# Query features scaled by the ratio of their two sums, in a two-layer linear-attention and gated-MLP kernel

## The chip, the core and the metric

The kernel runs on one core of a Trainium2 chip, as one launch. The metric is the device time of that launch in microseconds. Five engines work side by side, each through its own queue in order: TensorE (PE, matmuls; its weight loads are shown as PEld), VectorE (DVE), ScalarE (ACT), GpSimd (POOL), and SyncE (SP), which here issues transfers. An engine that waits for a semaphore holds up everything behind it in its queue.

## The reference

Two rounds of attention block and MLP block on x of 2048 tokens x 512, all in bf16. Cut to what matters:

```python
def _A_ref(x, wqkv, w_phi, wo):                      # H = 32 heads of Dh = 16
    q, k, v = split(x @ wqkv)
    pq = jnp.einsum("bhsd,hdf->bhsf", q, w_phi)
    pk = jnp.einsum("bhsd,hdf->bhsf", k, w_phi)
    phi_q = jnp.concatenate([_softmax(pq, axis=-1), _softmax(-pq, axis=-1)], axis=-1)
    phi_k = jnp.concatenate([_softmax(pk, axis=-1), _softmax(-pk, axis=-1)], axis=-1)
    kv = jnp.einsum("bhsf,bhsd->bhfd", phi_k, v)
    z  = jnp.einsum("bhsf->bhf", phi_k)
    num = jnp.einsum("bhqf,bhfd->bhqd", phi_q, kv)
    den = jnp.einsum("bhqf,bhf->bhq", phi_q, z)[..., None] + 1e-6
    return (num / den) reshaped to (B, S, D) @ wo
def _B_ref(x, W_gate, W_up, W_down):                 # F = 1376
    gate = relu(x @ W_gate); return (gate * (x @ W_up)) @ W_down
x = x + _A_ref(_layernorm(x), ...); x = x + _B_ref(_layernorm(x), ...)   # twice
```

Each row of a softmax has 16 entries. The output of a query is a quotient in which phi_q stands above and below.

## The kernel before

The 2048 tokens are 16 tiles of 128 rows. x stays in SBUF (`X`) from the first load to the last store, and so do all the weights. At the start `w_phi` is made block diagonal (`Wblk`, line 409, DVE) and folded into the key and query parts of `wqkv` (`fold`, lines 430 to 453): weights are turned (`turn`, line 440), copied (`wT`), multiplied by `Wblk` (line 448) and copied into `Wk2` and `Wq2` (`W2`). One matmul group then gives p itself.

For each of the two layers:

- `norm_A` (480): row statistics on DVE, their Ln and Exp on ACT, scaled rows `xn`, turned by a transposing transfer (`turn`, 461) or by PE (466).
- Keys, per tile (`Keys.begin` and `finish`, 531 to 578): `K` on PE (535); exp(p) and exp(-p) on ACT into the two halves of `ek` (538); 64 row sums of 16 entries on DVE (`sk`, 546); 1/sum as Exp(-Ln) on ACT (555, 558); the scaling of `ek`, two instructions of 512 columns on POOL or DVE (`halves`, 505 to 519, recorded under line 509); `V` on PE (541) with a copy `vext` by ACT or DVE (425, 426); `kvz` on PE (570), which adds the tile to the sums over all tokens in the one PSUM tile `q`.
- `build` (580): DVE masks these sums into `R`, which every query needs.
- Queries, per tile (`query`, 594 to 613): `Q` on PE (597), exp(p) and exp(-p) on ACT (600), 64 sums on DVE (`sq`, 603), Ln and Exp of all 64 on ACT (606, 608), the scaling of both halves (`phq`, two instructions of 512 columns, line 509 again), and a transposing transfer on SP (`fq`, 611) that waits for both.
- `attend` (616): `erq` on PE (622), the reciprocal of the denominator (`rden`), the product `o` on DVE (636), its transposition `oT`, `proj` on PE (645), and x plus it on DVE with row sums (`resS`, 649).
- `mlp` (655), in blocks of 1, 2 or 4 tiles: centred rows `xc` on DVE (665), turned into `xnTB`; `G` and `Up` on PE (722), relu on ACT (`rg`, 726), the product `hT` on DVE straight from PSUM (739) or after an ACT copy (741, 730), `down` on PE (762), x plus it on DVE (769), and the store in layer 1 (833).

What runs when is not found by a scheduler on the chip. Every step is an `Op` in a list; `ORDER` (181) is a written-out permutation of the list, and each engine's queue is that order cut down to its own steps. `PLACE` (152) says, bit by bit, which of a step's two engines is taken where it has an `alt`; `SLOTS` (158) names the buffer that each step takes. `IDLE` (169) says how many matmuls on zeros (line 419) PE does ahead of its first steps, on top of the eight of `warm`. Pools that matter here: six PSUM tiles `b` for all projections, 21 tiles `ek`, 5 `vext`, 4 `sk`, 4 `sq`, 7 `fq`.

Work of layer 1's keys stands among the MLP of layer 0, and PE does in all 8 + 6 matmuls on zeros, 512 for the four attention projections, 1,691 for the MLP, and the rest for sums, queries and turns.

Of the kernel before, what the change touches and what calls it, by code (L numbers as in the profile page):

```python
# [8 lines left out]
P = 128  # L9
# [133 lines left out]
class K:  # L143
# [9 lines left out]
    "0101110100000000001100000100110001000011010001111000000011001101010101001001001000101001111111011010"  # L153
    "1011110000000100000001001101000000000111011001011111010111000101001100000101111101001100001101010100"
    "1111111110101010010001000011000100000000101100101010100001001100011100010000110011001101000110111001"
    "010110010110111001110100110100000"
)
SLOTS = (
    "0001425210034050000151131234202310332121143404550125d3104c02302b3020a12113g533004002394131703202e141"
    "5i022124504f013k03583226105214413624335a011h100b033c05053623122j214910170400020501131002000245011020"  # L160
    "2500001142021002010100203200101143020002012105002004314023104g13300215112012320410311e34110200400450"
    "10205113120513d5100i42221240121321402422031200151030231042100142131004133610104f33242541002510104203"
    "51101520500512052130201550414201515300804024k2232c4020121152143124212004023502a533344112050010024104"
    "02024213011055002220j4203h05133317362b222f1506242i013a114023391638231c343e352k221d014g10011500020514"
    "0010124302000012011021450000121302100024010021050012201000011011521101530431102000005112025421011101"
    "0213125200125020013101050032154203115143114220221100253415210511200211401013403005210402213013222420"
    "500210300512431510432512113015114024105320310110512400202"
)
IDLE = (
    0, 0, 0, 0, 0, 0, 0, 0, 0, 0, 2, 0, 4, 0, 0, 0, 0, 0, 0, 0, 0,  # L170
# [108 lines left out]
def kernel(  # L279
# [11 lines left out]
    def new(name, shape, dt=BF16):  # L291
        return sb.tile([P] + shape, dt, name=name)
# [47 lines left out]
    def op(eng, cost, due, emit, deps=(), takes=(), uses=(), name="", **kw):  # L340
        o = Op(eng, cost, due, emit, deps, takes, uses, name, **kw)
        ops.append(o)
        return o
# [535 lines left out]
```

## Time and profile before

| what | value |
|---|---|
| three runs | 377.31 us median (377.04 to 377.71) |
| span of the profiled execution, first to last instruction | 375.3 us |
| DVE, ACT and POOL busy, 10 to 60 us | 49.8, 48.2 and 36.2 of 50 us |
| DVE, ACT and POOL busy, 66 to 200 us | 103.7, 65.5 and 15.5 of 134 us |
| DVE, ACT and POOL busy, 200 to 260 us | 55.9, 45.0 and 36.9 of 60 us |
| DVE, ACT and POOL busy, 260 to 372 us | 62.8, 39.0 and 2.2 of 112 us |

The page gives the profiled execution its span alone; the runs' times are 1.7 to 2.4 us longer, 2.0 us at the median, which is what lies around the span. PE's busy share is near 100% in nearly every stretch, and since its matmuls overlap (a 512-column matmul is shown with 379 ns, but the next one starts 216 ns later) busy time alone doesn't tell lost time; counts of matmuls times the distance of their starts do. The same holds in small for DVE and ACT, whose instructions overlap by about a tenth of a microsecond.

### The profile page before, as it was taken

What the parts mean: (1) busy time and instruction counts of PE and PEld (TensorE: products, weight loads), DVE (VectorE), ACT (ScalarE), POOL (GpSimd) and SP (SyncE); (2) the same over time, 40 slices, a digit from 0 to 9 for tenths busy, and PEclk for the clock granted to TensorE, in tenths of its full rate; (3) what the DMA queues carried; (4) which work ended last, traced back from release to release, by engine and by line L of the source; (5) the groups of instructions that cost most, each with busy time, mean ns of one, the idle gap of its engine ahead of it and who ended that gap; (6) DMA issues with size and microseconds to landing.
All of it is one profiled execution on the core that took longest, in us unless ns stands there. A gap on an engine that the chain in (4) does not pass through costs nothing.

```text
span 375.3 us, 7459 instructions
## 1 busy us (share of the span) xinstructions
PE 364.6 (97%) x2793; PEld 216.6 (58%) x2833; DVE 285.1 (76%) x596; ACT 209.7 (56%) x553; POOL 93.5 (25%) x91
## 2 busy tenths in 40 slices
PE   8989997999999999999999999999999999999996
PEld 4534454868554554466476555587745444558585
DVE  6999999999998673685767999999994755543322
ACT  6989999746464532265155499973425323414031
POOL 0377984341010102001004269774000000000000
PEclk9999999999999999999999999999999999999999
DMA  8858844769814221012020102968664120211110
GB/s 256 191 139 175 312 58 85 123 113 132 164 36 84 47 53 31 11 25 56 9 56 2 29 2 57 141 93 142 143 132 85 31 56 2 56 29 51 42 51 30
DMA packets 93444, 31.21 MB, mean 83 GB/s; under 512 B 85248, under 2 KB 92384, under 8 KB 93408
## 3 DMA queue, kind: packets, MB, share of 16 engines
q1 hardware_dynamic: 92992, 30.34, 39.5%
q8 instruction: 22, 0.36, 0.4%
q10 hardware_dynamic: 416, 0.39, 0.3%
q14 instruction: 14, 0.11, 0.1%
HBM read 7.91 MB, written 2.10 MB: 27 GB/s over the span
## 4 chain that ended last, share of the span: by engine, by line
PE 90%; ACT 6%; DVE 1%; POOL 1%; issue 1%; DVEq 0%; another core or an unknown queue 0%
PE b L722 37%; PE b L762 20%; PE b L645 7%; PE b L541 6%; PE b L535 6%; PE b L597 6%; PE b L698 3%; PE q L622 2%; PE q L570 2%; ACT ek L600 1%; POOL ek L509 1%; ACT ek L538 1%; PE q L419 1%; DVE sq L603 1%; ACT hT L425 1%
## 5 line engine op out<-in xcount | busy, mean ns | idle before, releaser
L722 PE MATMUL b<-xnTB,wgu 128*128 128x128 bf16 (+2 forms) x1200 | 149.6, 279 | 0.0
L722 PEld LDWEIGHTS <-wgu 128*128 128x128 bf16 x1200 | 97.1, 98 | 43.6
L509 POOL TENSOR_TENSOR ek<-ek,sk 128x512 bf16<-128x512 bf16 x47 | 51.0, 1109 | 135.5 <-ACT sk L558 108.2
L726 ACT ACTIVATE gu<-b 128x512 bf16<-128x512 f32 (+1 forms) x83 | 47.8, 580 | 64.9 <-PE b L722 64.6
L762 PE MATMUL b<-wd,hT 128*128 128x512 bf16 (+2 forms) x350 | 81.3, 372 | 0.7
L762 PEld LDWEIGHTS <-hT 128*128 128x128 bf16 (+1 forms) x363 | 34.6, 98 | 35.9 <-DVE hT L739 0.2
L509 POOL TENSOR_TENSOR ek<-ek,sq 128x512 bf16<-128x512 bf16 x38 | 42.0, 1127 | 32.6 <-ACT sq L608 18.0
L739 DVE TENSOR_TENSOR hT<-gu,b 128x512 bf16<-128x512 bf16 (+1 forms) x44 | 29.6, 676 | 18.5 <-PE b L722 16.9
L546 DVE TENSOR_REDUCE sk<-ek 128x64 f32<-128x1024 bf16 x32 | 38.7, 1210 | 5.3 <-ACT ek L538 5.2
L538 ACT ACTIVATE ek<-b 128x512 bf16<-128x512 f32 x64 | 35.9, 598 | 9.2 <-PE b L535 8.0
L603 DVE TENSOR_REDUCE sq<-ek 128x64 f32<-128x1024 bf16 x32 | 38.2, 1207 | 0.3 <-POOL ek L509 0.3
L600 ACT ACTIVATE ek<-b 128x512 bf16<-128x512 f32 x64 | 36.1, 623 | 0.6 <-PE b L597 0.5
L730 DVE TENSOR_TENSOR hT<-gu 128x512 bf16<-128x512 bf16 (+1 forms) x39 | 16.7, 429 | 22.5 <-ACT gu L741 22.3
L769 DVE SCALAR_TENSOR_TENSOR X<-b,rsB,X 128x512 bf16<-128x512 f32 (+1 forms) x33 | 23.2, 726 | 13.5 <-PE b L762 13.4
L645 PE MATMUL b<-wo,oT 128*128 128x512 bf16 x118 | 31.2, 379 | 1.2 <-ACT oT L425 0.7
L535 PE MATMUL b<-Wk,xnTA 128*128 128x512 bf16 x122 | 31.4, 379 | 0.3
L541 PE MATMUL b<-wv,xnTA 128*128 128x512 bf16 x124 | 31.0, 379 | 0.4 <-ACT xnTA L425 0.2
L597 PE MATMUL b<-Wq,xnTA 128*128 128x512 bf16 x121 | 30.5, 379 | 0.3
L741 ACT CAST gu<-b 128x512 bf16<-128x512 f32 (+1 forms) x39 | 21.7, 558 | 15.0 <-PE b L722 14.6
L649 DVE SCALAR_TENSOR_TENSOR X<-b,X 128x512 bf16<-128x512 f32 x32 | 21.8, 682 | 3.5 <-PE b L645 3.4
L636 DVE TENSOR_TENSOR o<-q,rd 128x512 bf16<-128x512 f32 x32 | 21.9, 685 | 0.8 <-ACT rd L633 0.6
L477 DVE BATCH_NORM_STATS2 bstA<-X 128x6 f32<-128x512 bf16 x32 | 21.0, 681 | 1.9 <-DMA X<-in_A_x_dram 1.8
(71 smaller groups left out, 349.1 us busy)
## 6 DMA issues: line engine op xcount, KB each, us to landing
out_dram<-X SPq DMA_DIRECT2D x15, 128.0 KB, 1.7
X<-in_A_x_dram SPq DMA_DIRECT2D x6, 256.0 KB, 4.8
wgu<-in_B_W_gate_dram SPq DMA_DIRECT2D x4, 344.0 KB, 4.0
wgu<-in_B_W_up_dram SPq DMA_DIRECT2D x4, 344.0 KB, 3.6
wd<-in_B_W_down_dram SPq DMA_DIRECT2D x5, 256.0 KB, 3.6
wv<-in_A_wqkv_dram SPq DMA_DIRECT2D x2, 256.0 KB, 4.3
wo<-in_A_wo_dram SPq DMA_DIRECT2D x4, 128.0 KB, 3.2
fq<-ek SPq DMA_TRANSPOSE x32, 3.3
```

The lines of the kernel that those rows point to most:

```text
L509: e.tensor_tensor(out=out().rearrange("p g s (h f) -> p (g s h) f", f=DH)[:, lo:lo + n], in0=ek.t[:].rearrange("p g s (h f) -> p (g s h) f ...
L535: k = op("PE", mm(4, 512), due, lambda: [nc.tensor.matmul(kp.t[:], lhsT=xnTA[c][:, i, b, :], rhs=Wk2[:, b, :], start=(b == 0), stop=(b == ...
L538: e = [op("ACT", act(512), due, lambda s=s: nc.scalar.activation(out=ek.t[:, :, s, :], in_=kp.t[:].rearrange("p (g e) -> p g e", e=GQ), fu ...
L541: v = op("PE", mm(4, 512), due_v, lambda: [nc.tensor.matmul(vp.t[:], lhsT=xnTA[c][:, i, b, :], rhs=wv[:, b, :], start=(b == 0), stop=(b == ...
L546: a = op("DVE", SUM16, due, lambda: nc.vector.tensor_reduce(out=sk.t[:, row, :], in_=ek.t[:].rearrange("p g s (h f) -> p (g s h) f", f=DH) ...
L597: q = op("PE", mm(4, 512), due, lambda: [nc.tensor.matmul(qp.t[:], lhsT=xnTA[c][:, i, b, :], rhs=Wq2[:, b, :], start=(b == 0), stop=(b == ...
L600: e = [op("ACT", act(512), due, lambda s=s: nc.scalar.activation(out=ek.t[:, :, s, :], in_=qp.t[:].rearrange("p (g e) -> p g e", e=GQ), fu ...
L603: a = op("DVE", SUM16, due, lambda: nc.vector.tensor_reduce(out=sq.t[:], in_=ek.t[:].rearrange("p g s (h f) -> p (g s h) f", f=DH), axis=A ...
L645: a = op("PE", mm(4, 512), due + 3, lambda j=j, yp=yp: [nc.tensor.matmul(yp.t[:], lhsT=oT.t[:, j, b, :], rhs=wo[:, b, :], start=(b == 0), ...
L722: nc.tensor.matmul(ps.t[:, q * W:(q + 1) * W].rearrange("p (i t) -> p i t", t=P), lhsT=wgu[:, s, b, g * P:(g + 1) * P], rhs=xT.t[:, 0:n, b ...
L726: nc.scalar.activation(out=gu.t[:, 0, 0:cols], in_=gp.t[:, 0:cols], func=AF.Relu)
L762: nc.tensor.matmul(yp.t[:, 0:c1 - c0], lhsT=h.t[:m, f * W + i * P:f * W + (i + 1) * P], rhs=wd[:m, f, c0:c1], start=(f == 0), stop=(f == N ...
```

## The change

For queries alone, the common factor of phi_q may be chosen freely, since it stands above and below in the quotient (but for the 1e-6). Both softmaxes are multiplied by the sum of exp(-p): the half exp(-p) stays as it is, and the half exp(p) is multiplied by the ratio of the sum of exp(-p) to the sum of exp(p). Ln and Exp are done on 32 sums in place of 64, a small product makes the ratio (`rat`), and one instruction of 512 columns scales (`phq`) in place of two. Keys are scaled as before, both halves.

`w_phi` is centred: the mean over the 16 entries of each row of a head's matrix is taken off ahead of `Wblk`, by two small DVE instructions. A softmax doesn't see a constant shift of p, but the ratio of both sums does.

`ORDER`, `PLACE`, `SLOTS` and `IDLE` are new throughout, so all engines' queues are in a new order, transfers at the start too. Line numbers of the changed file are 4 to 16 higher after the edits. The diff, cut to its core:

```diff
 IDLE = (
-    0, 0, 0, 0, 0, 0, 0, 0, 0, 0, 2, 0, 4, 0, 0, 0, 0, 0, 0, 0, 0,
+    0, 5, 0, 3, 0,
 )
...
+    cmean = new("cmean", [NB], F32)
...
-    c_blk = op("DVE", dve(512), 20, lambda: nc.vector.tensor_tensor(
-        out=Wblk[:].rearrange("p b (j f) -> p b j f", f=DH),
-        in0=wf[:].unsqueeze(2).to_broadcast([P, NB, HB, DH]),
-        in1=Mf[:].unsqueeze(1).unsqueeze(3).to_broadcast([P, NB, HB, DH]), op=Alu.mult), [c_m, l_wf], name="Wblk", port=True)
+    def blocks():
+        nc.vector.tensor_reduce(out=cmean[:], in_=wf[:], axis=AX.X, op=Alu.add)
+        nc.vector.scalar_tensor_tensor(out=wf[:], in0=cmean[:].unsqueeze(2).to_broadcast([P, NB, DH]),
+                                       scalar=-1.0 / DH, in1=wf[:], op0=Alu.mult, op1=Alu.add)
+        nc.vector.tensor_tensor(
+            out=Wblk[:].rearrange("p b (j f) -> p b j f", f=DH),
+            in0=wf[:].unsqueeze(2).to_broadcast([P, NB, HB, DH]),
+            in1=Mf[:].unsqueeze(1).unsqueeze(3).to_broadcast([P, NB, HB, DH]), op=Alu.mult)
+
+    c_blk = op("DVE", (900, 1000), 20, blocks, [c_m, l_wf], name="Wblk", port=True)
...
+        pos, neg = (lambda: sq.t[:].rearrange("p (g s h) -> p g s h", s=2, h=HG)[:, :, 0, :],
+                    lambda: sq.t[:].rearrange("p (g s h) -> p g s h", s=2, h=HG)[:, :, 1, :])
         a = op("ACT", RLN[0], due, lambda: nc.scalar.activation(
-            out=sq.t[:], in_=sq.t[:], func=AF.Ln, scale=1.0), [a], (), [sq], name="lnq")
+            out=pos(), in_=pos(), func=AF.Ln, scale=1.0), [a], (), [sq], name="lnq")
         a = op("ACT", REXP[0], due, lambda: nc.scalar.activation(
-            out=sq.t[:], in_=sq.t[:], func=AF.Exp, scale=-1.0), [a], (), [sq], name="rq")
-        a = halves("phq", ek, lambda: ek.t[:], lambda lo, n: sq.t[:, lo:lo + n], PHI["POOL"], due, [a], [], [ek, sq])
+            out=pos(), in_=pos(), func=AF.Exp, scale=-1.0), [a], (), [sq], name="rq")
+
+        def ratio(e):
+            e.tensor_tensor(out=pos(), in0=pos(), in1=neg(), op=Alu.mult)
+
+        def scale(e):
+            v = ek.t[:, :, 0, :].rearrange("p g (h f) -> p g h f", f=DH)
+            e.tensor_tensor(out=v, in0=v, in1=pos().unsqueeze(3).to_broadcast([P, NG, HG, DH]), op=Alu.mult)
+        a = op("POOL", (150, 200), due, lambda: ratio(nc.gpsimd), [a], [], [ek, sq], name="rat", port=3,
+               alt=("DVE", DVE0, lambda: ratio(nc.vector), 1))
+        a = op("POOL", (1016, 1058), due, lambda: scale(nc.gpsimd), [a], [], [ek, sq], name="phq", port=3,
+               alt=("DVE", dve(512), lambda: scale(nc.vector), 1))
         a = op("SP", XWIDE, due, lambda: nc.sync.dma_start_transpose(
-            out=fq.t[:], in_=ek.t[:].rearrange("p g s e -> p (g s e)")), a, [fq], [ek], name="fq", move=1450)
+            out=fq.t[:], in_=ek.t[:].rearrange("p g s e -> p (g s e)")), [a], [fq], [ek], name="fq", move=1450)
```

How the instructions lie on the engines under the two lists (where the counts differ; the rest is alike, and PE's matmuls are the same but for two more on zeros):

| step | before | after |
|---|---|---|
| scaling of queries, 512 columns | POOL 38, DVE 26 | POOL 20, DVE 12 |
| ratio, 32 columns | none | POOL 26, DVE 6 |
| scaling of keys, 512 columns | POOL 47, DVE 17 | POOL 46, DVE 18 |
| copy `vext` | ACT 19, DVE 13 | ACT 27, DVE 5 |
| copy of `Up`, with the product from SBUF | ACT and DVE 39 each | ACT and DVE 45 each |
| product straight from PSUM | DVE 44 | DVE 38 |
| squares for the MLP's norm | ACT 21, DVE 11 | ACT 17, DVE 15 |
| matmuls on zeros | 14 | 16 |

More of the change, by code (lines that the diff above doesn't have):

```diff
@@ L152 @@
 PLACE = (
[L153 to L156, printed above, removed]
+    "0101010000000000001100000000110100010010000000000001000111101101000000011000000100011000100001000010"
+    "0001101000011000000011010100110001110011101011010011100001000110100001110000000011101111000101000110"
@@ L157 @@
+    "0100101000110000010010101010110110000100001000001000101010000110101101111000000111000001000110100011"
+    "011001110110111010101101110111101"
 )
 SLOTS = (
[L159 to L167, printed above, removed]
+    "000142513003310100244050111133321252122025040573132314333j40011h5431f43010k5115732225b5031822105g512"
@@ new lines @@
+    "0e0211220444003a31291206043d2348355f061i102c01122535343g03003653220e104b0100000001151102000241011020"
+    "0400001145021020410000123400001121021002430202002005421414514434102511115110223502200g30210000200042"
+    "13135014210512k1434152201221121301142322111322131220420152020150532054013f2321292104c010200100200005"
+    "5112144032011211232143023242054108431332230224101e343214112011321113003520142003321b0010050020021231"
+    "12225413351444410000h5310h143d061j23370256051i101a3153261j045d1337250f003c32352146161804010204021214"
@@ L168 @@
+    "0000123502100030010021020010121502000034011021320002301105211111201322000240402000101511522511011501"
+    "1223013010003212001005132043044035141150143221033001102021112201314213312302304425114521403124115324"
+    "100100120451550252010350201114103421412311400411522430105"
 )
 IDLE = (
-    0, 0, 0, 0, 0, 0, 0, 0, 0, 0, 2, 0, 4, 0, 0, 0, 0, 0, 0, 0, 0,
+    0, 5, 0, 3, 0,
 )
```

183 rows, old and new, of the table ORDER are left out of this document.

## The prediction

> **What bounds the kernel now.** First the page's busy times:
>
> ```profile
> span 375.3 us, 7459 instructions
> ...
> PE 364.6 (97%) x2793; PEld 216.6 (58%) x2833; DVE 285.1 (76%) x596; ACT 209.7 (56%) x553; POOL 93.5 (25%) x91
> ```
>
> PE is the bound, but 97% of busy time doesn't say how much it loses. For that, PE's instructions in order of time, columns start and length:
>
> ```profile
> 1.34 3.60 PE L419 MATMUL q<-zero 128*128 128x512 bf16 x8 [1.34 <-DVE zero L396]
> 4.72 0.90 PE L440 MATMUL b<-ident,hT 128*128 128x128 bf16 x12
> ...
> 10.04 1.03 PE L419 MATMUL q<-zero 128*128 128x512 bf16 x4
> ...
> 12.30 1.04 PE L541 MATMUL b<-wv,xnTA 128*128 128x512 bf16 x4
> ```
>
> ```profile
> 158.41 1.80 PE L722 MATMUL b<-xnTB,wgu 128*128 128x256 bf16 x15
> ...
> 362.21 4.18 PE L722 MATMUL b<-xnTB,wgu 128*128 128x128 bf16 x72
> ...
> 368.88 3.22 PE L762 MATMUL b<-wd,hT 128*128 128x512 bf16 x25
> ```
>
> From start to start a 512-column matmul takes 0.2156 us (four at 10.04: 1.03 less the last one's 0.379, over 3), one of 256 columns 0.109 (1.80 less 0.273, over 14), of 128 0.0556 (4.18 less 0.219, over 71); line 698's 192 columns 0.0823 by the same reckoning, the 65 and 68 columns of the sums and queries 0.032. By the matmuls in the queue: 1187 x 0.2156 + 422 x 0.109 + 128 x 0.0823 + 584 x 0.0556 + 512 x 0.032 = 361.4 us of gapless stream. PE starts at 1.34 and ends at 372.1, so it loses 370.76 - 361.4 = 9.4 us. That, and no more, is what an order can win; 3.2 us of tail (to 375.3) and the 1.34 stand beside it.
>
> Where the 9.4 lies: ahead of the V at 12.30 the queue has 22 matmuls of 512 and 48 of 128 columns, 7.4 us, so 12.30 - 1.34 - 7.4 = 3.55 are lost by then, 1.7 of it because the first eight take 0.4225 each ((4.72 - 1.34) / 8). Next the waits from 10 to 66 us (total, times, longest):
>
> ```profile
> PEld L570 <- POOL ek L509: 2.8, 4, 0.8
> ...
> PEld L466 <- DVE xn L665: 1.0, 1, 1.0
> PEld L645 <- ACT oT L425: 0.8, 1, 0.8
> ...
> PEld L466 <- DVE o L636: 0.7, 1, 0.7
> ```
>
> The key sums wait for the scaling on POOL at 19 to 25 us; the distances of the matmul starts give 2.3 us. The turn into layer 0's MLP at 59 to 64 us waits for `o`, `oT` and `xc`: 2.5 us. Some 1.0 is scattered. Who is behind, the busy times in stretches show (PE, PEld, DVE, ACT, POOL):
>
> ```profile
> 0.00:12.00 12.00, 10.16 (x69) 5.18 (x70) 8.14 (x30) 8.41 (x21) 0.70 (x6) 1.00 0.89 273
> 12.00:28.00 16.00, 14.18 (x104) 7.10 (x104) 16.00 (x32) 14.74 (x46) 10.13 (x10) 1.00 0.63 138
> 28.00:58.00 30.00, 29.79 (x225) 15.40 (x228) 29.92 (x40) 29.41 (x84) 25.95 (x24) 1.00 0.71 175
> ...
> 200.00:260.00 60.00, 59.53 (x531) 36.08 (x538) 55.94 (x87) 44.96 (x131) 36.88 (x34) 1.00 0.41 68
> ```
>
> DVE doesn't rest from 12 to 58 us: there it sets the pace, with ACT close by. From 200 to 260 all are as full, yet PE loses 0.5.
>
> **The change, part by part.** PE's stream: two more matmuls on zeros, +0.4, so 361.8. `zero` is DVE's first instruction now (behind two memsets of 0.075 before), so PE starts at about 1.15.
>
> Start. Thirteen zeros stand ahead of the first turn. The slow ones ended between 4.72 and 4.96 here: nine at 0.4225 and four at 0.2156 give 1.15 + 3.8 + 0.9 = 5.85; if all thirteen are slow, 6.65. I take 5.85, since that row shows the time of the turn-over, and keep 0.8 for the range. The Trainium skill (TensorE: Matmul & The Clock Gate, Part 1) says the slow phase is a span of about 3.4 us of activity and not a count of matmuls; by that the zeros end at 5.85, by a count at 6.65 with 0.8 on the sum, and this trace, with 3.4 us for eight, fits both. Then ACT sets the pace: its first copy can start 0.45 after the first turn (4.72 to 5.22 before), at 6.3, and ahead of the last `Wk2` copy it has nine copies at 0.48 (start to start, from four in 2.05 us) and four small ones, 0.57 in all: 11.2, and K at 11.3. K's place in the stream is 7.62 (24 of 512, 44 of 128 columns), so the loss is 11.3 - 1.15 - 7.6 = 2.55 in place of 3.55: **-1.0**, and -0.2 for the earlier start.
>
> Centring: two instructions on 64 columns; DVE's small rows (0.08 to 0.12 start to start) give 0.2. The load of `w_phi` goes from second to fourth place on SP, each place 0.5 us: landing 5.16 before, about 6.2 now, `Wblk` ready at 6.2 + 0.2 + 0.7 = 7.1. PE reaches the fold at 5.85 + 20 turns x 0.056 + 3 zeros = 7.6, so nothing, with 0.5 of cover. The second half of w_k is issued on ACT behind the table load (1.28) now: landing 5.0 before, at most 6.3, needed at 6.9. Both are covered by the thirteen zeros. On SP the first turned pair for keys stands behind nine loads and four weight turns, much as before (12.95), and lands near 15; its K comes at 13.9 + 3.7 = 17.6.
>
> The middle, to the first turn of `xc` in layer 0. Start to start DVE takes about 0.08 less than a row's mean, ACT 0.12 less. Ahead of that `xc`, DVE's queue held 105 instructions before and holds 97 now. Common are 16 each of statistics (0.60), their sums (0.09), `xn` (0.33) and `sk` (1.13), 34.4 us. Beside them before: 9 `sq` (1.13), 11 of 512 columns (0.60), 9 scalings (0.62 to 0.65), small ones 0.9: 58.0. After: 7 `sq`, 8 of 512 columns, 5 scalings (keys only), `rden`, `rat`, centring and small ones 1.4: 51.8. DVE had idled 3.9 by 58 us, 58.0 + 3.9 = 61.9, and the `xc` ran at 62.77: such a sum is right within 1 us. Now: 51.8 + 4.1 (its idle time by the first `sk`, reckoned as above: 11.9 of work when that comes up at 16.0) + 0.35 = 56.3. ACT's queue to the same point goes from 56.0 to 51.8 (seven fewer exponentials at 0.48, four fewer pairs of Ln and Exp, three more `vext`): 51.8 + 4.7 idle = 56.5. PE's stream to `xnTB` is 53.24 (53.67 before): 1.15 + 53.24 + 2.55 = 56.9, against 63.18 now. So DVE no longer holds PE; the three come level.
> POOL: the first sum's place moves from 12.6 to 18.2 in the stream, the second from 14.6 to 20.2, which ends the 2.3 of waits. POOL starts the keys at about 19.4 and has 27 scalings at 1.05, one `rat` and one `phq` ahead of the last sum: 49.0, needed at 51.6.
> Unshown prices: `rat` on POOL lies between 0.10 (its memset of one column) and 1.05 (512 columns); I take 0.2, since it has 32 columns. `phq` on every second 64 columns: 1.05 to 2.1 on POOL (if gaps count), 0.62 to 1.24 on DVE; I take the low ends, the columns being as many as in the row. At both high ends POOL has 1.9 more ahead of the last sum, inside its 2.6. Ln and Exp of 32 sums: 0.19 to 0.26 (line 629, 606).
> Level queues still collide: before, DVE's own sum gave 61.9 and PE came at 63.18, 1.3 later. I add the same: 56.9 + 1.3 = 58.2, a loss of 3.8 by `xnTB` in place of 63.18 - 1.34 - 53.67 = 8.2: **-4.4**.
>
> The rest lost 9.4 - 8.2 = 1.2. In the second turn the last K stands 8.3 us ahead of the last sum in the stream (9.6 before); its own chain is 2 x 0.48 + 1.2 + 2 x 0.27 + 2 x 1.06 and hand-overs, some 5.5, so it fits with less room: **+0.5**. Copies moved from DVE to ACT (8 `vext`, 4.8 us) lie under PE there.
>
> Sum: 1.15 + 361.8 + 3.8 + 1.7 + 3.2 = 371.65 us of span. The median run is 377.31 - 375.3 = 2.0 longer than the profiled span: **373.6**.
>
> **Rivals.**
> *The collisions go too.* PE is at `xnTB` by 56.9: 372.3. For it: POOL and DVE have room; against: ACT has 0.4.
> *The gain is largely given back*: three level engines wait for each other's short steps (the last sum to the first `erq` is 0.9 us of stream now, 2.6 before, and `R`, `Rz` between them take 0.85 with hand-overs), and half of the 4.4 returns: 375.8, to 377.7 if all does.
> *ACT becomes the bound, slower.* It gets `vext` and relu copies. Before xnTB it must do 51.8 us; each us of idleness beyond 5 goes to PE one for one. In 0 to 58 us it idled 3.6 + 1.3 + 0.6 = 5.4. If its Ln and Exp steps, which wait for DVE sums, hold the copies behind them so that it idles over 10.5 us, the stall is that of before and more: 378.5. Against: seven exponentials fewer.
> *The change doesn't do what it says*: strided halves cost as much as whole ones, 12 on DVE 0.6 dearer, 20 on POOL 1.05. Ahead of `xnTB` DVE has none of them; up to 1.0 later: 374.6, within the forecast's range.
>
> **Numbers.** Forecast 0.58 (its own range 371.5 to 375.7: 0.8 for the slow zeros, 1.0 for dear halves, the collisions either way); without collisions 0.15; given back 0.17; ACT 0.10. A measurement here tells 0.2%, 0.75 us, from no change. Faster: 0.58 + 0.15 + half of 0.17 = 0.81; same 0.08; slower 0.11. Range 371.0 to 377.4.
>
> **What would show it.** PE's first turn near 5.9; the first K near 11.3; PE's waits for POOL ahead of the first key sums under 0.3; `xnTB`'s turn at 57 to 59 us; DVE with idle time between 12 and 58; the last matmul near 368.5. I am wrong if PE waits for ACT's copies through 20 to 50 us, or if the sums at 222 to 226 us wait for `ek`.

## The result, and where the time went

The changed kernel takes 386.60 us at the median (four runs, 386.19 to 389.21), the kernel before beside it 377.26 (377.04 to 377.71): a ratio of 1.0255, 95% interval 1.0235 to 1.0275. It is slower by 9.3 us, where 373.6 was forecast. The page of the changed kernel begins, with PE's granted clock by fortieths of the span last:

```profile
span 384.3 us, 7396 instructions
...
PE 366.7 (95%) x2790; PEld 217.5 (57%) x2835; DVE 287.4 (75%) x592; ACT 208.2 (54%) x558; POOL 82.5 (21%) x98
...
PEclk9999989999999999999999999999999999999999
```

DVE is busy 2.3 us longer than before (285.1) although it has less to do, and one slice of PE's clock is an 8; before, all were 9. PE's instructions in order of time run from 1.19 to 381.14 us, 379.95 for a gapless 361.8: it loses 18.2 us where it lost 9.4. By stretch, from the distances of the matmul starts, less the gapless distance of each (the columns sum to 0.1 to 0.5 more than these totals):

| stretch, us | lost before | lost after |
|---|---|---|
| 0 to 30 (start, first key sums) | 5.9 | 2.7 |
| 30 to 50 | 0.0 | 0.8 |
| 50 to 70 (last key sums, turn to the MLP) | 2.7 | 5.9 |
| 70 to 220 | 0.4 | 3.0 |
| 220 to 250 (the same in layer 1) | 0.4 | 4.1 |
| 250 to the end | 0.5 | 1.8 |

The start is close to the forecast. Start, length, engine, line, and idle time with its releaser, for PE:

```profile
1.19 4.36 PE L423 MATMUL q<-zero 128*128 128x512 bf16 x13 [1.19 <-DVE zero L394]
5.38 0.61 PE L444 MATMUL b<-ident,hT 128*128 128x128 bf16 x8
...
7.80 0.84 PE L452 MATMUL b<-Wblk,hT 128*128 128x128 bf16 x12 [0.49 <-DVE Wblk L411]
...
10.94 1.24 PE L539 MATMUL b<-Wk,xnTA 128*128 128x512 bf16 x5
```

The first K comes at 10.94 (forecast 11.3), and the four waits of the first key sums for POOL are gone. The busy times by stretch answer to the ones before (PE, PEld, DVE, ACT, POOL, clock, DMA share, GB/s):

```profile
12.00:28.00 16.00, 15.63 (x99) 7.80 (x100) 15.93 (x31) 15.45 (x44) 6.27 (x6) 1.00 0.73 155
28.00:58.00 30.00, 25.75 (x206) 13.78 (x209) 29.02 (x34) 25.87 (x79) 27.64 (x28) 0.95 0.61 158
...
200.00:260.00 60.00, 56.28 (x534) 35.17 (x542) 54.42 (x82) 42.36 (x116) 24.96 (x24) 1.00 0.27 51
```

From 28 to 58 us PE falls from 29.8 to 25.8, with DVE nearly as full as before (29.0). PE there, then DVE and POOL at the same time:

```profile
52.77 0.42 PE L574 MATMUL q<-vext,ek 128*128 128x65 bf16 x8
55.70 1.94 PE L574 MATMUL q<-vext,ek 128*128 128x65 bf16 x32 [2.51 <-DVE ek L513]
57.86 1.20 PE L601 MATMUL b<-Wq,xnTA 128*128 128x512 bf16 x3 [0.22 <-issue]
```

```profile
50.62 5.01 DVE L513 TENSOR_TENSOR ek<-ek,sk 128x512 bf16<-128x512 bf16 x4
```

```profile
49.44 5.00 POOL L513 TENSOR_TENSOR ek<-ek,sk 128x512 bf16<-128x512 bf16 x4
```

The key sums wait for key scalings on DVE: four of them, 2.6 us by the row the prediction used, take 5.0 while POOL does four of its own. And the 32 matmuls of 65 columns that follow take 1.94 us (1.19 in a run below at full clock): the clock record reads a half from 55.22 to 58.63 us. Earlier in the same stretch the `xn` on DVE, short instructions with one SBUF input, had met POOL's scalings too: the two in this row take 1.46 us, where the prediction's 0.33 from start to start gives about 0.74.

```profile
33.73 1.46 DVE L499 TENSOR_SCALAR xn<-X,mvA,rsA 128x512 bf16<-128x512 bf16 x2
```

Layer 1 has the like:

```profile
227.31 0.40 PE L470 MATMUL b<-ident,xn 128*128 128x128 bf16 x4 [1.62 <-DVE xn L499]
...
238.47 0.43 PE L574 MATMUL q<-vext,ek 128*128 128x65 bf16 x8 [0.39 <-POOL ek L513]
239.48 0.68 PE L574 MATMUL q<-vext,ek 128*128 128x65 bf16 x16 [0.59 <-POOL ek L513]
240.69 0.94 PE L574 MATMUL q<-vext,ek 128*128 128x65 bf16 x24 [0.52 <-ACT vext L429]
```

**A measure for it.** For every DVE instruction that overlaps one of POOL's products in time, take its length less the median of the same instruction and shape without one beside it, and sum what exceeds 0.06 us. The kernel before loses 4.0 us of DVE time in this way, in 14 instructions; the changed one 15.9 us in 24. That sum, "the collisions" below, is DVE's time, not PE's. Up to the turn of `xc` in layer 0 the changed kernel loses 5.2 us of it, the kernel before 0.6.

### The profile page after: what moved, and what is told of

Read it like the earlier page. It is cut to its first block, busy times and chain, and to the rows that moved or that the text cites. A ratio compares the mean times of both kernels' runs of the same rounds, so it can differ in the third digit from the quotient of the medians.

```text
span 384.3 us, 7396 instructions
## 1 busy us (share of the span) xinstructions
PE 366.7 (95%) x2790; PEld 217.5 (57%) x2835; DVE 287.4 (75%) x592; ACT 208.2 (54%) x558; POOL 82.5 (21%) x98
## 5 line engine op out<-in xcount | busy, mean ns | idle before, releaser
L738 PE MATMUL b<-xnTB,wgu 128*128 128x128 bf16 (+2 forms) x1200 | 152.8, 279 | 1.1 <-DMA xnTB<-xn 1.0
L778 PE MATMUL b<-wd,hT 128*128 128x512 bf16 (+2 forms) x341 | 83.6, 372 | 1.1
L513 POOL TENSOR_TENSOR ek<-ek,sk 128x512 bf16<-128x512 bf16 x46 | 51.6, 1146 | 117.3 <-DVE bstA L481 70.9
L755 DVE TENSOR_TENSOR hT<-gu,b 128x512 bf16<-128x512 bf16 (+1 forms) x38 | 25.4, 669 | 26.0 <-ACT gu L742 16.6
L542 ACT ACTIVATE ek<-b 128x512 bf16<-128x512 f32 x64 | 37.2, 613 | 9.4 <-PE b L539 9.3
L604 ACT ACTIVATE ek<-b 128x512 bf16<-128x512 f32 x64 | 35.9, 602 | 5.3 <-PE b L601 5.2
L550 DVE TENSOR_REDUCE sk<-ek 128x64 f32<-128x1024 bf16 x32 | 37.9, 1207 | 0.1
L601 PE MATMUL b<-Wq,xnTA 128*128 128x512 bf16 x120 | 31.8, 382 | 1.7 <-ACT vext L429 1.0
L757 ACT CAST gu<-b 128x512 bf16<-128x512 f32 (+1 forms) x45 | 24.8, 567 | 14.7 <-PE b L738 14.1
L746 DVE TENSOR_TENSOR hT<-gu 128x512 bf16<-128x512 bf16 (+1 forms) x45 | 18.9, 426 | 13.7 <-ACT gu L757 13.6
L622 POOL TENSOR_TENSOR ek<-ek,sq 128x512 bf16<-128x512 bf16 x20 | 21.9, 1101 | 15.2 <-DVE sq L618 14.6
```

The costliest lines, as they stand in the source:

```text
L513: e.tensor_tensor(out=out().rearrange("p g s (h f) -> p (g s h) f", f=DH)[:, lo:lo + n], in0=ek.t[:].rearrange("p g s (h f) -> p (g s h) f ...
L542: e = [op("ACT", act(512), due, lambda s=s: nc.scalar.activation(out=ek.t[:, :, s, :], in_=kp.t[:].rearrange("p (g e) -> p g e", e=GQ), fu ...
L550: a = op("DVE", SUM16, due, lambda: nc.vector.tensor_reduce(out=sk.t[:, row, :], in_=ek.t[:].rearrange("p g s (h f) -> p (g s h) f", f=DH) ...
L601: q = op("PE", mm(4, 512), due, lambda: [nc.tensor.matmul(qp.t[:], lhsT=xnTA[c][:, i, b, :], rhs=Wq2[:, b, :], start=(b == 0), stop=(b == ...
L604: e = [op("ACT", act(512), due, lambda s=s: nc.scalar.activation(out=ek.t[:, :, s, :], in_=qp.t[:].rearrange("p (g e) -> p g e", e=GQ), fu ...
L738: nc.tensor.matmul(ps.t[:, q * W:(q + 1) * W].rearrange("p (i t) -> p i t", t=P), lhsT=wgu[:, s, b, g * P:(g + 1) * P], rhs=xT.t[:, 0:n, b ...
```

## The experiments

Twelve kernels ran. Theory A: the order found anew lays DVE's and POOL's scalings side by side, they exclude one another, and PE waits for them. Against it: the arithmetic is dear (B), DVE is late or slow for another reason (C), the order's tight turns by DMA (D).

### Arithmetic and order apart

`arith_old_order`: the changed arithmetic under `PLACE`, `SLOTS`, `IDLE` and `ORDER` of the kernel before.

```diff
 IDLE = (
-    0, 5, 0, 3, 0,
+    0, 0, 0, 0, 0, 0, 0, 0, 0, 0, 2, 0, 4, 0, 0, 0, 0, 0, 0, 0, 0,
 )
```

> The changed arithmetic (ratio, half scaling, centring) under the order, the placement and the buffers of the kernel before, with each ratio ahead of its query scaling; 22 of 32 query scalings then lie on DVE, and POOL scales keys as before. Theory A (the time was lost by the order found anew: its side-by-side scalings on DVE and POOL, its tight turns by DMA): 374 to 378 us, ratio to the kernel before 0.992 to 1.002. Rival B (the arithmetic itself is dear, its ratio step adds a stage to every query's chain, whatever the order): 382 us or more.

`old_arith_new_order`: the reverse, the new lists with the old scaling, whose two halves take the places of `rat` and `phq`.

```diff
-        a = op("POOL", (150, 200), due, lambda: ratio(nc.gpsimd), [a], [], [ek, sq], name="rat", port=3,
-        a = op("POOL", (1016, 1058), due, lambda: scale(nc.gpsimd), [a], [], [ek, sq], name="phq", port=3,
...
+        a = halves("phq", ek, lambda: ek.t[:], lambda lo, n: sq.t[:, lo:lo + n], PHI["POOL"], due, [a], [], [ek, sq])
```

> The arithmetic of the kernel before (both halves of the queries scaled, two scalings for each) under the changed kernel's order, placement and buffers. Theory A: the order keeps its own losses and gets longer steps besides, 385 to 394 us. Rival B: the order is fine and the arithmetic was the loss, 376 to 380 us.

| | old order | new order |
|---|---|---|
| old arithmetic | 377.5, collisions 4.0 | 394.4, collisions 25.1 |
| new arithmetic | 377.85, collisions 0.8 | 386.6, collisions 15.9 |

(1.0009, 0.9995 to 1.0023, and 1.0447, 1.0421 to 1.0473, against the kernel before.) The order costs 9 us with the new arithmetic and 17 with the old. The arithmetic gains 8 us under the new order, where it takes scalings out of the collisions, and nothing under the old one: POOL is busy 70 us there instead of 93 and DVE 281.8 instead of 285.1, but PE waits at the same places as before. In PE's order of time, first the kernel before, then `arith_old_order`:

```profile
60.95 1.04 PE L645 MATMUL b<-wo,oT 128*128 128x512 bf16 x4 [0.68 <-ACT oT L425]
...
63.18 0.40 PE L466 MATMUL b<-ident,xn 128*128 128x128 bf16 x4 [0.84 <-DVE xn L665]
```

```profile
61.44 1.04 PE L661 MATMUL b<-wo,oT 128*128 128x512 bf16 x4 [0.81 <-ACT oT L429]
...
63.66 0.40 PE L470 MATMUL b<-ident,xn 128*128 128x128 bf16 x4 [0.93 <-DVE xn L681]
```

The waits are no shorter with less work on POOL and DVE: the saved work lay off the path.

### The collision by itself

`side_by_side` runs five kinds of DVE instruction, four in a row: alone, then POOL's four scalings alone, then both released together.

```diff
+        for f in (two, tiny, one, frompsum, total):
+            sc = gate(p)
+            for k in range(4):
+                f(p, k, sc)
+            sc = gate(p + 1)
+            pool4(p + 1, sc)
+            sc = gate(p + 2)
+            pool4(p + 2, sc)
+            for k in range(4):
+                f(p + 2, k, sc)
+            p += 3
```

> Not the reference's computation: five kinds of DVE instruction, four in a row, first alone, then POOL's four scalings alone, then both released together. Theory A (a DVE instruction with only SBUF operands and a POOL scaling exclude one another for the whole of an instruction, in turns): beside POOL, DVE's scalings with two SBUF inputs go from 0.60-0.70 us to about 1.4-1.55 for those that start while POOL works, the tiny products of 128x32 from 0.17 to about 1.0, the one-input scalings of 512 from 0.35-0.40 to about 1.1, and POOL's from 1.06 to 1.1-1.6; the products out of PSUM and the reductions stay within 5%, and so does POOL beside these. Rival C (shared bandwidth): all kinds slow alike and in proportion to their length, the tiny ones by under 0.1 us, reductions as well.

Its timeline of both engines (`two`: two SBUF inputs; `tiny`: two of 32 columns; `one`: one SBUF input; `frompsum`; `total`: the reduction):

```profile
2.64 2.50 DVE L40 TENSOR_TENSOR two<-src,sc 128x512 bf16<-128x512 bf16 x4
...
5.26 4.09 POOL L40 TENSOR_TENSOR pool<-src,sc 128x512 bf16<-128x512 bf16 x4 [4.82 <-DVE sc L33]
...
10.11 5.08 DVE L40 TENSOR_TENSOR two<-src,sc 128x512 bf16<-128x512 bf16 x4
10.15 5.95 POOL L40 TENSOR_TENSOR pool<-src,sc 128x512 bf16<-128x512 bf16 x4 [0.80 <-DVE sc L35]
...
16.86 0.50 DVE L55 TENSOR_TENSOR tiny<-sc 128x32 f32<-128x32 f32 x4
...
22.89 2.22 DVE L55 TENSOR_TENSOR tiny<-sc 128x32 f32<-128x32 f32 x4
...
34.75 4.45 DVE L59 TENSOR_SCALAR one<-src,sc 128x512 bf16<-128x512 bf16 x4
...
39.83 2.49 DVE L40 TENSOR_TENSOR frompsum<-ps,sc 128x512 bf16<-128x512 f32 x4
...
47.85 2.48 DVE L40 TENSOR_TENSOR frompsum<-ps,sc 128x512 bf16<-128x512 f32 x4
...
62.62 4.59 DVE L67 TENSOR_REDUCE total<-src 128x64 f32<-128x1024 bf16 x4
```

Alone, the two series take 2.50 and 4.09 us; together they end after 6.0, so 0.6 is all that side by side saves. One by one, DVE's scalings took 0.69, 1.54, 1.54 and 1.54 us, POOL's 1.56, 1.50, 1.50 and 1.50: strict turns. The `tiny` ones took 0.19, 1.05, 0.18 and 1.04 us (0.18 alone): the wait doesn't depend on the length of the instruction but on what POOL has begun. One input of 512 columns goes from 0.41 to between 1.14 and 1.25. Products out of PSUM and reductions aren't touched, nor is POOL beside them. So theory A holds and a shared bandwidth doesn't. The Trainium skill (SBUF — State Buffer, section "SBUF: two separate sides") says the same: DVE, with two SBUF inputs or in its two-port modes, and GpSimd hold a shared pair of ports as an exclusive lock for a whole instruction. This trace agrees, with 0.69 against 1.54 us.

### POOL's part taken out

`pool_short`: four key scalings and one query scaling on POOL, from 49.4 us on, cut short. This kernel and the next leave that work out, so they don't compute the reference.

```diff
         for k, e in enumerate(engs):
+            n = 2 if len(ops) in (235, 236, 170, 181) else H
...
-                    "POOL": ("POOL", (1016, 1058), lambda k=k: phi(nc.gpsimd, k * H, H), 3)}
+                    "POOL": ("POOL", (1016, 1058), lambda k=k, n=n: phi(nc.gpsimd, k * H, n), 3)}
```

> The changed kernel with POOL's four key scalings of 49.4 to 54.4 us cut to 2 of their 32 blocks and the query scaling behind them to 1 of 8 groups; the work left out is not done elsewhere. Theory A (scalings of DVE and POOL slow one another): DVE's four key scalings of 50.6 to 55.6 take 0.65 to 0.72 us each instead of 0.73 to 1.54, together 2.7 to 2.9 instead of 5.0; PE's wait of 2.5 us before the key sums falls below 0.6, no half clock follows, and the time falls by 3 to 5 us (381.5 to 383.5). Rival C (DVE is simply late, or its scalings are long for the tiles they read): they stay near 1.25 us on average, the wait stays over 2, the time within 1 us.

384.26 us (383.47 to 385.52). DVE's row:

```profile
51.88 2.64 DVE L513 TENSOR_TENSOR ek<-ek,sk 128x512 bf16<-128x512 bf16 x4
```

2.64 us for the four as expected; PE's wait before the key sums falls to 0.31 (2.67 by the same distance of starts in the changed kernel), the half clock at 55 us is gone. By the first residual sum the kernel is 2.25 us ahead of the changed one, though this execution's zeros ended later and had put it 1.26 behind: 3.5 gained. It isn't all kept. In layer 1, after waits like those shown above, PE runs at half clock in this execution, which the changed kernel's did not there:

```profile
238.82 3.51 PE L602 MATMUL b<-Wq,xnTA 128*128 128x512 bf16 x8
```

Eight matmuls take 3.51 us in place of 1.89. The time, 2.3 us down, lies 0.8 above what was expected.

`pool_all_short`: every scaling on POOL cut in this way.

```diff
-            ways = {...
-                    "POOL": ("POOL", (1016, 1058), lambda k=k: phi(nc.gpsimd, k * H, H), 3)}
+                    "POOL": ("POOL", (1016, 1058), lambda k=k: phi(nc.gpsimd, k * H, 2), 3)}
...
-        a = op("POOL", (1016, 1058), due, lambda: scale(nc.gpsimd), [a], [], [ek, sq], name="phq", port=3,
+        a = op("POOL", (1016, 1058), due, lambda: scale(nc.gpsimd, 1), [a], [], [ek, sq], name="phq", port=3,
```

> The changed kernel with every scaling on POOL cut, keys to 2 of 32 blocks and queries to 1 of 8 groups; nothing is done elsewhere. Summed over the profile, DVE's instructions that ran beside POOL's took 15.9 us more than the same ones alone (before: 4.0). Theory A (collisions are what the new order lost by): that sum falls below 3 us, the waits at 53.0, 225.5 and 237.9 to 240 (6.3 us) fall to under 2 together, time 378 to 381.5 us. Rival D (the order's turns by DMA and its tight queues cost most, whatever POOL does): the waits for DMA stay, and the time stays over 383.

376.49 us, 0.9973 of the kernel before (0.9958 to 0.9988): 10.1 us off, more than expected. The collisions fall to 0.25 us. PE's rows at the key sums and the turn of layer 0, then at the key sums of layer 1, and the one large wait that stays:

```profile
51.95 1.74 PE L574 MATMUL q<-vext,ek 128*128 128x65 bf16 x40
...
59.54 0.40 PE L470 MATMUL b<-ident,xn 128*128 128x128 bf16 x4
```

```profile
229.11 2.22 PE L574 MATMUL q<-vext,ek 128*128 128x65 bf16 x56
...
259.36 2.79 PE L738 MATMUL b<-xnTB,wgu 128*128 128x256 bf16 x24 [1.45 <-DMA xnTB<-xn]
```

The waits at 53.0, 225.5 and 237.9 to 240 are 0.3, 0 and 0.3; the waits for `oT` by DMA at 74 to 110 us, 1.6 in the changed kernel, are 0.2, so these came from `o` and `xc` being late on DVE, not from the transfers. Only the wait for `xnTB` is D's, 1.6 (1.2 in the changed kernel). 10.1 us is an upper bound of what collisions cost, since POOL's own length is gone as well; of that, PE's waits for POOL in layer 1 were 1.3. No run of the new order keeps POOL's work and takes the collisions alone away.

### The half clock, and sharing undone

`zeros_in_wait`: twelve matmuls of zeros in the wait at 53 us.

```diff
+            if o is ops[249]:
+                for _ in range(12):
+                    nc.tensor.matmul(p_b.tiles[3][:], lhsT=zero[:, 0:P], rhs=zero[:], start=True, stop=True)
```

> The changed kernel with twelve matmuls of zeros (12 x 0.216 = 2.6 us) on PE in its wait at 53.0 to 55.7 us, into a free bank. Theory A says that the half clock of 55.2 to 58.6 us is started by this wait and costs some 1.7 us of its own: with PE busy the record of half clock is gone and the time falls by 1.4 to 2.0 us (384.6 to 385.2). Rival: the half clock has another cause, or what follows waits for DVE and POOL anyway: time within 0.5 us of the changed kernel's 386.6.

```profile
53.78 2.75 PE L866 MATMUL b<-zero 128*128 128x512 bf16 x12
56.46 1.19 PE L574 MATMUL q<-vext,ek 128*128 128x65 bf16 x32
```

The half clock is gone from the record and the sums run at full speed, but the time isn't lower: 387.62 us (386.12 to 388.16). In the profiled execution a wait of 1.2 us for `fq` at 68 us follows, its first key sum on DVE stands 0.76 later than the changed kernel's, and the span is 384.1 against 384.3. Of its four runs two had a clock of 1.000 (386.12, 387.52) and two 0.996. So its time doesn't show what the half clock costs. By the reckoning used for `pool_short`, the first residual sum stands 0.37 us earlier although the zeros ended 0.77 later: an estimate of 1.1 us gained there, and the wait at 68 us takes it back. The changed kernel's own runs go the same way, 386.19 us at a mean clock of 0.996 and 389.21 at 0.991, but which of the two brings the other isn't shown.

`place_by_lock`: six key scalings of layer 1 exchanged between the engines, by six bits of `PLACE`.

```diff
-    "0001101000011000000011010100110001110011101011010011100001000110100001110000000011101111000101000110"
-    "0100101000110000010010101010110110000100001000001000101010000110101101111000000111000001000110100011"
+    "0001101000011000000011010100110001110011101011010011100001010110100001110000000011101111001100000110"
+    "0100100000110000001010101010110110000100001000001000101010000110101101111000000111000001000110100011"
```

> The changed kernel with six key scalings of the second layer placed anew and nothing else: two that DVE does alone at 228 to 231 us go to POOL, idle there, and the four that POOL does at 233.9 to 239.4 beside DVE's go to DVE. Theory A (scalings exclude one another, so that the faster engine does them sooner alone: 7 x 0.60 = 4.2 us against the 5.5 of both together): PE's waits of 237.9 to 240 us (2.0) fall to 0.3-1.2 and the time by 0.6 to 1.8 us (384.8 to 386.0). Rival C (the sharing of work still pays): the waits grow to 3 or more, 387.5 or more.

388.81 us (386.88 to 390.15): the time lies in rival C's range, PE's waits in neither theory's. Two of the four runs had a mean clock of 0.991; the two at 0.996 took 386.88 and 388.06, the changed kernel's at 0.995 and 0.996 386.24 and 386.19. DVE in order of time:

```profile
225.77 2.22 DVE L499 TENSOR_SCALAR xn<-X,mvA,rsA 128x512 bf16<-128x512 bf16 x2
...
234.61 2.50 DVE L513 TENSOR_TENSOR ek<-ek,sk 128x512 bf16<-128x512 bf16 x4 [0.26 <-ACT sk L562]
...
238.35 3.09 DVE L513 TENSOR_TENSOR ek<-ek,sk 128x512 bf16<-128x512 bf16 x5
```

Alone, DVE does its scalings at 0.62 each, and PE's waits from 238 us on come to 2.05 (2.0 with the sharing): POOL's help shows no worth there, and its absence wins nothing. The scalings moved to POOL at 225.7 now meet the two `xn` (2.22 us, 1.48 in the changed kernel), and PE's wait there grows from 1.8 to 2.5. A collision was moved, not removed.

### The centring

`no_centring`:

```diff
-        nc.vector.tensor_reduce(out=cmean[:], in_=wf[:], axis=AX.X, op=Alu.add)
-        nc.vector.scalar_tensor_tensor(out=wf[:], in0=cmean[:].unsqueeze(2).to_broadcast([P, NB, DH]),
-                                       scalar=-1.0 / DH, in1=wf[:], op0=Alu.mult, op1=Alu.add)
```

> The changed kernel without the two instructions that centre w_phi; the shift cancels in the quotient. The profile of the changed kernel shows PE waiting 0.65 us for Wblk at 7.1 us, behind these two. Theory A (centring is on PE's path there, and the stretch to 50 us carries it on): 0.3 to 0.7 us faster, 385.9 to 386.3. Rival (hidden, as the prediction had it, or taken up by the next wait): within 0.2 us of 386.6.

388.72 us (387.82 to 389.51): not faster. The fold waits as long without it, now for the copy ahead of it:

```profile
9.53 0.62 PE L449 MATMUL b<-Wblk,hT 128*128 128x128 bf16 x8 [0.49 <-ACT hT L426]
```

This profile has two stretches of half clock where the changed kernel's has one, and its zeros ended at 6.71 us in place of 5.38; runs of this order spread by 2 to 3 us, so a few tenths can't be read from their times. The changed kernel's own profile says more: the copy that the fifth fold matmul reads ended at 7.97 us, and that matmul ran at 8.02, right behind the four that had waited for `Wblk`. Without that wait it could not have run sooner.

### Edits that should have won, and did not

In `turn_reordered` the changed arithmetic keeps the old order but for the turn at 51 to 66 us; `start_reordered` moves three projections at 20 to 26 us as well. The core of the first, as steps of `ORDER` (480 is the first `erq`, 471, 426, 462 and 417 are Q):

```diff
-399 Q, 471 Q, 426 Q, 480 erq, 462 Q, 417 Q, 484 oT, 486 proj, 488 erq
+399 Q, 480 erq, 471 Q, 426 Q, 484 oT, 462 Q, 486 proj, 488 erq, 417 Q
```

> The changed arithmetic under the old order, with two local edits at the turn to the first MLP: five query scalings of 51 to 66 us go from DVE to POOL, which idles there from 55, and the first denominator matmul is put ahead of two Q projections, which then fill PE's later waits for the o copy and for xc. PE lost 2.5 us at 60 to 64 us in that order. Theory A (nothing but the order of the work keeps the changed arithmetic from a gain): this loss falls to 0.5-1.2, time 375.8 to 377.0 us. Rival B (ACT and DVE, full there, pass the wait on): time within 0.5 us of 377.85.

> As the run before it, and at 20 to 26 us two V and one Q projection go ahead of key sums that wait for POOL's scalings (2.3 us in the old order), and one more query scaling goes from DVE to POOL. Theory A: these waits fall below 0.8 and the gain stays where DVE's queue allows it, another 0.5 to 1.8 us, time 374.3 to 376.5. Rival B (DVE, busy all of 12 to 58 us, sets the end of this stretch): PE waits later by what it won, time within 0.4 us of the run before it.

381.55 (381.18 to 382.07) and 382.47 us (381.57 to 383.20), slower than either theory allowed. In the first, G came at 63.25 instead of 64.73, of which 0.5 is an earlier start of that execution, and then, DVE and PE in order of time:

```profile
68.23 1.22 DVE L611 TENSOR_REDUCE sq<-ek 128x64 f32<-128x1024 bf16 x1 [4.38 <-POOL ek L626]
```

```profile
70.10 0.61 PE L642 MATMUL q<-R,fq 128*128 128x68 bf16 x8 [3.33 <-DVE o L656]
```

The sum waits for its tile `sq`, which a scaling that had gone to POOL still read; `o` stands behind it on DVE, and the next `erq` needs the PSUM tile that `o` empties. The second has the same wait; what it gains at 20 to 26 us, later waits take again, and more. Two further rounds moved what was found late; the core of the first of them:

```diff
-480 erq, 384 sq, 483 o, 429 sq, 402 sq, 499 o
+480 erq, 483 o, 384 sq, 429 sq, 499 o, 495 resS, 402 sq
```

> The edited old order once more. In turn_reordered the changed turn reached the first G at 63.25 us (64.73 in arith_old_order), but DVE then stood 4.4 us before a query sum whose tile a POOL scaling still held, and a denominator matmul 3.3 us behind it. Here that sum is put behind the next residual sum, its predecessors' small steps earlier, the first o ahead of a query sum, and the oT turn and the projection ahead of one more Q. Theory A: PE loses 0.8 to 1.5 us at 55 to 72 us (2.6 in arith_old_order), time 376.0 to 377.0, ratio to the kernel before 0.995 to 0.999. Rival B: another wait takes the place, 377.5 or more.

> The edited old order a third time: in turn_reordered2 PE lost 4.0 us at 55 to 72, of it 1.0 before a projection whose bank two late exponentials held, 1.5 before a denominator matmul behind a query sum and a reciprocal, 0.6 before the first oT turn. Here the projection has another bank, the query sum stands behind the o that is waited for, and one Q stands ahead of the oT turn again. Theory A (the changed arithmetic gains once the order gives its freed time to what PE waits for): PE loses 1.0 to 2.0 us there, time 375.8 to 377.0, ratio to the kernel before 0.995 to 0.999. Rival B: the wait moves on once more, 377.6 or more.

379.67 (378.63 to 379.82; 1.0051, 1.0038 to 1.0064) and 379.78 us (379.39 to 380.02; 1.0056, 1.0042 to 1.0069). The last one loses 0.4 us at 50 to 60, but 2.0 at 60 to 70 and 2.3 at 70 to 80, for `hT`, `xnTB`, `fq` and `oT`, each in its turn. Collisions are 0.84 in both, so these are plain order: the wait moved on each time, and rival B was right. No kernel that leaves nothing out beat the one before; whether the changed arithmetic can gain under yet another order stays open.

## Why the prediction was wrong

The span came out 12.7 us above the forecast's 371.65: the turn of `xc` stood at 63.87 us, not at 58.2 (5.7), and the rest took 7.0 more.

- *PE is the bound, 361.8 gapless; the start gains 1.2.* Right: the first turn stood at 5.38 (5.85), the first K at 10.94 (11.3), POOL's four waits of 2.3 us are gone. That the start came out so near is partly luck: with the same thirteen zeros the first turn stood at 6.71 and the first K at 12.42 in `pool_all_short`. (The 6.65 is the time with all thirteen slow; a count of eight slow ones would give 5.6.)
- *Centring costs nothing, 0.5 of cover.* The cover wasn't there: PE waited 0.49 us for `Wblk`. The cost was nothing all the same, since the copy next in line came 0.2 us later than `Wblk`.
- *Prices not shown.* `rat` is 0.25 us on POOL (0.2 taken), `phq` 1.06 and 0.69 at the median (the low ends): right.
- *"5 scalings (keys only)" on DVE at 0.62 to 0.65.* **The step that failed.** The four ahead of the last key sums took 5.0 us and not 2.6, because POOL's four ran beside them, and five `xn` at 20 to 34 us, summed at 0.33 each, lost another 2.5 to POOL's scalings. The two queues were summed each for itself, and whether they could run at once wasn't asked. *"Level queues still collide: I add the same", 1.3,* is where it should have stood, and it was carried over from an order in which DVE lost 0.6 us to POOL up to this turn to one in which it loses 5.2. On PE, 6.7 us were lost from 30 us to the turn where 1.3 was allowed; the largest parts are 2.7 before the key sums, 1.5 in the slow stretch behind them, and 1.1 for a `vext` copy at 51 us that is gone in `pool_all_short`. Between 12 and 58 us DVE was idle for 1.0 us and ACT for 4.7, so the queues did not come level, and DVE still set the pace. Without collisions the sum was good: in `pool_all_short` the turn came at 59.54, of it 0.9 because the zeros ended at 6.71 and not at 5.85; that leaves 58.7, against 58.2.
- *POOL done at 49.0, needed at 51.6.* Its last four key scalings ended at 54.4: from 19.3 us on it stood idle 4.4 us for 1/sum from ACT, which the sum had left out, and the collisions lengthened the last four by 0.8 together (5.0 against 4.2 for four elsewhere). Without the 0.8 they would have ended at 53.6, an estimate, and PE, which stood idle from 53.2 on, would still have waited some 0.4 us for POOL; the rest of its 2.5 us there is DVE's.
- *The rest, "+0.5" for the second turn.* Lost: 4.1 from 220 to 250 us, 3.0 from 70 to 220, 1.8 after. With collisions gone the part behind the `xc` turn takes 315.3 us (forecast 313.45, changed kernel 320.5), so 5.1 of the 7.0 went with them. Even that kernel took 376.49 us, 2.9 above the forecast: 0.9 for the late zeros, 0.5 up to the turn and 1.9 behind it are not collisions.
- *Rivals.* "Given back" had the sign of the gain's loss but no price above 377.7 (its own sum, 373.6 + 4.4, gives 378.0); "ACT becomes the bound" is not what happened: ACT was busy 25.9 of 30 us at 28 to 58. None of them was two engines excluding each other.

The trace of before held a sign: a POOL scaling took 1.06 us at the median and 1.57 at most, DVE's 0.68 and 1.10, for the same columns (count, then shortest, median and longest in ns, first and last start in us):

```profile
L509 POOL TENSOR_TENSOR ek<-ek,sk x47: 1049/1057/1565, 14.5 to 230.6; 128x512 bf16<-128x512 bf16 x47
...
L509 DVE TENSOR_TENSOR ek<-ek,sk x17: 620/681/1097, 35.7 to 211.5; 128x512 bf16<-128x512 bf16 x17
```

## What to carry to other kernels

Queue sums hold for engines that can run at once. Where a trace shows one instruction at two lengths, find what ran beside it, and sum the two engines as one queue wherever the new order lays such instructions side by side (here products and scalings whose operands all lie in SBUF, not products out of PSUM and not reductions). Sharing them saved 0.6 of 6.6 us; giving them to the faster engine is the obvious answer, but the one run that did so, `place_by_lock`, was no faster, since it moved a collision elsewhere. And saved work is worth what the order makes of it: here the same arithmetic was worth 8 us under one order and nothing under another.

## What the runs showed of the hardware

- DVE and POOL take turns by whole instructions, and length is no shelter: two of four DVE products of 32 columns took 1.05 us instead of 0.18, and a scaling of two elements in the changed kernel (line 699) 1.04.
- PE's clock fell to half for 3.41 us nine times in the profiles of these kernels: in all six with a single idle time of 2.5 us or more (2.5 to 3.3), 2.0 to 4.7 us after it had begun, and in three of the six with waits in pieces among the short key sums of layer 1, where the same pieces of 0.4 to 0.6 us had it in one execution and not in the next (one of the three, `old_arith_new_order`, had a wait of 1.3 us among them). An idle time of 2.35 us had none. The Trainium skill (TensorE: Matmul & The Clock Gate, Part 1) puts such a fall down to an idle window of about 3.4 us. The length of the slow stretches agrees; the idle times here were shorter.
- The slow phase at the start isn't a fixed time either: of the same thirteen zeros six and most of a seventh were slow in the changed kernel's profile (2.5 to 2.9 us from PE's first matmul), and all thirteen in `pool_all_short` (5.5 us).
